# Rows of o as 64 by 64 products on quarters of the array

## Chip, core and metric

The kernel runs on one core of a Trainium2 chip. The metric is the device time of one execution, in microseconds (us). The median of four runs before the change is 909.13 us (908.34 to 909.99).

## The reference

Linear attention over 8 batches, 8 heads, 576 positions and 64 columns a head, then a two-layer network with softplus over the 4608 rows. All inputs and results are float32 to the caller; the inputs of the network's weights arrive in eight bytes a number and are made float32 in the kernel.

```python
def _attn_ref(q, k, v, g_norm):
    kv = np.einsum('bhsd,bhse->bhde', k, v)
    out = np.einsum('bhsd,bhde->bhse', q, kv)
    rms = np.sqrt(np.mean(out * out, axis=-1, keepdims=True) + 1e-06)
    return (out / rms * g_norm).astype(np.float32)

def _moe_ref(x, w_in, w_out):       # x: (B,H,S,D) -> (B*S, H*D) = (4608, 512)
    h = x @ w_in                    # (4608, 2048)
    g = np.maximum(h, 0.0) + np.log1p(np.exp(-np.abs(h)))
    return (g @ w_out).astype(np.float32)
```

## The kernel before

**The network.** The 4608 rows are 12 blocks of 384, each three tiles of 128. The 2048 hidden columns are 16 chunks of 128. The work goes in three phases over the chunks, and in each phase over all blocks; one block with one chunk is a step, and there are 192 steps. To keep float32 accuracy in the fast format fp32r, x, the hidden values and both weights are each split into three terms. A step is one group of 12 products into a bank h (L647), the softplus on ScalarE (L667), the split of its result on ScalarE and VectorE (L669, L658, L662), and three groups of three products into the banks s0, s1, s2 (L654), one for each tile of the block. At the end of a phase `leave` takes the sums out and adds those of the phase before.

**The attention.** For each batch `kv_of` multiplies k by v (L495): five groups of eight float32 products, each of 128 by 64 on one half of the array's columns, halves in turn. A float32 product is two instructions in the trace. The result, 64 by 64 for each head, is copied by two instructions (L499) to `kv_diag`: four blocks of 128 by 128, one for a pair of heads, with zeros off the diagonal. `rows(t)` makes one tile of 128 rows of o: q of the tile, turned so that its columns are in the partitions, times the four blocks of `kv_diag` (L509). Of each product half the multiplications are by the zeros. A tile whose rows lie in two batches (tiles 4, 13, 22, 31) takes four products for each of them, on 64 columns of weights each. Then come the square (L577, ScalarE), the sum by head (L514, VectorE), the power -1/2 (L517, L518, GpSimd) and the scaling, called the norm (L521, VectorE). The product with g_norm is made in the split of x.

**Turning.** For tiles of batches 0 and 1 q is turned on TensorE (L564) and copied (L571); later ones are turned by VectorE (L539). The first 12 tiles of x are turned on TensorE (L526) and copied (L586). The first six go from there into the split of x (L438, L441, L445) as well; all others are stored to DRAM and loaded again by `x_again` (L625), once for each phase.

**Weights.** `weight` loads a chunk's weights (L276), makes float32 of them on VectorE and ScalarE (L287 to L317) and splits them (L349 to L371). For the first four chunks two products with the identity (L367, L368) help in the split.

**The order.** Nothing is ordered by hand: `add` records a task with its engine, an estimated cost in ns, the tasks it follows, a position `pos`, and the slots it takes and gives back. `Plan.order` walks through time and picks for each engine, among the tasks that could start soonest, the one with the least position. The places of a buffer are a ring: `m` has 13 places in SBUF shared by all loads and most temporaries; in PSUM there are h (2), o (2), tp (1), s0, s1, s2 (1 each), eight banks. `P0` holds 40 numbers from which the positions are made. Loads and stores are all issued by the queue on SyncE (SP), in the planned order. Where TensorE would be idle for 400 ns, `plan.spare` puts in a product with the identity (L763) whose result nobody reads, until the first L647.

Of the kernel before, what the change touches and what calls it, by code (L numbers as in the profile page):

```python
# [8 lines left out]
F32 = mybir.dt.float32  # L9
# [9 lines left out]
P = 128  # L19
# [21 lines left out]
class Plan:  # L41
# [3 lines left out]

    HANDOVER = {"PE": 250, "ACT": 120, "DVE": 120, "POOL": 150, "SP": 0}
    READY = {"PE": 2500, "ACT": 2500, "DVE": 4000, "POOL": 2500, "SP": 700}
    BEGIN = 4000
    SOON = 150

# [17 lines left out]
    def order(self):  # L68
        waiting = {id(t): len(t.after) + (t.follows is not None) for t in self.tasks}
        users = {}  # L70
        for t in self.tasks:
            for a in t.after + ([t.follows] if t.follows else []):
                users.setdefault(id(a), []).append(t)
        ready = {}
        for t in self.tasks:
            if not waiting[id(t)]:
                t.ready = 0
                ready.setdefault(t.engine, []).append(t)
        free = {r: [(0, i) for i in range(n)] for r, n in self.rings.items()}
        engine_free = dict(self.READY)  # L80
        dma_free = 1500
        last_read = {}
        done, left = [], len(self.tasks)
        while left:
            best = None
            for engine, tasks in ready.items():
                options = []
                for t in tasks:
                    at = max(engine_free[engine], t.ready)
                    if t.size:  # L90
                        at = max(at, dma_free - 2500)
                    for i, s in enumerate(t.take):
                        others = sum(u.ring == s.ring for u in t.take[:i])
                        if len(free[s.ring]) <= others:
                            break
                        at = max(at, sorted(free[s.ring])[others][0])
                    else:
                        options.append((at, t))
                if not options:
                    continue  # L100
                first = min(at for at, _ in options)
                at, t = min(((at, t) for at, t in options if at <= first + self.SOON),
                            key=lambda o: (o[1].pos, o[0]))
# [12 lines left out]
            if t in ready[t.engine]:  # L116
                ready[t.engine].remove(t)
                left -= 1
            for s in t.take:
                place = min(free[s.ring])  # L120
                free[s.ring].remove(place)
                s.place = place[1]
            t.start = at
            engine_free[t.engine] = at + t.ns
            t.end = at + t.ns + self.HANDOVER[t.engine]
            if t.size:
                dma_free = max(dma_free, at + t.ns) + t.size
# [12 lines left out]
        return sorted(done, key=lambda t: t.start)  # L140
# [3 lines left out]
def kernel(  # L144
# [39 lines left out]
    PLACES = 8  # L184
    LAST = PHASES[-1]

    P0 = [-83.5, -6.7, -71.3, -7.7, -12.6, -28.5, -9.9, 1.7, -54.5, -35.3, -53.7, -10.7, -25.7, -1.2,
          -3.7, -2.2, 0.5, -14.0, 12.5, 9.5, 5.5, 6.0, -2.0, 2.5, 2.5, 19.0, 0.5, 14.5, 8.5, 44.5, 49.5,
          68.0, 52.5, 73.0, 96.5, 100.0, 115.5, 110.5, 114.0, 8.5]
    CONVERT, FETCH, EARLY, LATER = P0[:8], P0[8:16], P0[16:27], P0[27:]  # L190
    BY_PE = 12
    AT_ONCE = 2 * TB
# [2 lines left out]
    const = ctx.enter_context(tc.tile_pool(name="const", bufs=1))  # L195
    sb = ctx.enter_context(tc.tile_pool(name="sb", bufs=1))
    ps = ctx.enter_context(tc.tile_pool(name="ps", bufs=1, space=PSUM))
    dram = ctx.enter_context(tc.tile_pool(name="dram", bufs=1, space=DRAM))

    ident_r = const.tile([P, P], F32R, name="ident_r")  # L200
# [6 lines left out]
    tails = [const.tile([P, H, D], F32, name=f"tail{i}") for i in range(2)]  # L207
    over = const.tile([P, 2 * KF], F32, name="over")
    scale = const.tile([P, 1], F32, name="scale")
    kv_diag = [const.tile([P, NP, P], F32, name=f"kv_diag{i}") for i in range(2)]  # L210


    rings = dict(m=13, xv=2, gv=2, g=2, raw=2, sq=1, 
                 tail0=1, tail1=1, qa=1, xb=1, x=2, r=2,
                 h=2, o=2, tp=1, s0=1, s1=1, s2=1)
    rings.update({f"w{i}_{c}": 1 for i in range(2) for c in range(PLACES)})
    PS = {"h", "o", "tp", "s0", "s1", "s2"}
    plan = Plan(rings)
    slot, add = plan.slot, plan.add

    def new(s, shape, dtype=F32):
        pool = ps if s.ring in PS else sb
        s.tile = pool.tile(shape, dtype, tag=f"{s.ring}_{s.place}", name=f"{s.ring}_{s.place}")
        return s.tile
# [241 lines left out]
    def kv_of(b):  # L466
# [1 line left out]


        pos = x_pos(first_tile[b]) - (EARLY[4] if b else EARLY[5])  # L470
        bank = slot("o")
        last = None
        MAIN = 4 * P
        for p in range(NP + 1):
# [14 lines left out]
            def run(ks=ks, vs=vs, p=p, tail=tail):  # L489
                kv = new(bank, [P, NP, D]) if p == 0 else bank.tile  # L490
                for i in range(4):
                    for e in range(2):
# [2 lines left out]
                        nc.tensor.matmul(kv[e * D:(e + 1) * D, i if tail else p], lhsT=l, rhs=r,  # L495
                                         start=(p == 0 and i == 0), stop=tail, skip_group_check=True)
            last = add("PE", 600, run, lds + [last], pos + 0.5 * p, [bank] if p == 0 else [], [ks, vs])
        kvd = kv_diag[b % 2]
        kv_ready[b] = [add("ACT", 360, lambda r=r: nc.scalar.copy(kvd[r:r + D, :, r:r + D], bank.tile[r:r + D]),  # L499
                           [last] + o_tasks.get(b - 2, []), pos + 2.5, [], [bank]) for r in (0, D)]  # L500

    def rows(t):
        pos = x_pos(t)
        tp, qT, o, x, r, xp, xg = (slot(n) for n in ("tp", "m", f"s{t}" if t < TB else "o", "x", "r", "tp", "m"))
        def out_rows():
            y = new(o, [P, H, D])
            for b, r0, n, _ in parts(t):
                for p in range(NP):
                    nc.tensor.matmul(y[r0:r0 + n, p::NP], lhsT=qT.tile[:, p, r0:r0 + n],  # L509
                                     rhs=kv_diag[b % 2][:, p].rearrange("r (h d) -> r h d", d=D),  # L510
                                     start=(p == 0), stop=True, skip_group_check=True)

        def reduce():
            nc.vector.tensor_reduce(out=new(r, [P, H]), in_=x.tile, axis=AX.X, op=ALU.add)  # L514
# [3 lines left out]
            nc.gpsimd.tensor_tensor(out=r.tile, in0=r.tile, in1=half, op=ALU.pow)  # L518

        def norm():  # L520
            nc.vector.tensor_tensor(out=x.tile, in0=o.tile, in1=r.tile.unsqueeze(2).to_broadcast([P, H, D]), op=ALU.mult)  # L521

        def turn_x():
            y = new(xp, [P, KD, P])
# [9 lines left out]
        for b, r0, n, s0 in parts(t):  # L534
# [23 lines left out]
                    return q_s.tile  # L558
                return q_s.tile[:, t * d_model:(t + 1) * d_model].rearrange("s (h d) -> s h d", d=D)

            def turn_q(n=n, q_s=q_s, at_qa=at_qa, tp=slot("tp")):
                y = new(tp, [P, NP, P])
                for p in range(NP):
                    nc.tensor.transpose(y[:, p, :n], pairs(natural(q_s, at_qa)[:n], p), ident[:n, :n])  # L564
# [6 lines left out]
            turned.append(add("ACT", 590, lambda n=n, r0=r0, tp=tp: nc.scalar.copy(part_of_qT(n, r0), tp.tile[:, :, :n]),  # L571
                              [a], pos - 1, [qT] if not r0 else [], [tp], follows=turned[-1] if turned else None))
        need = [u for pt in parts(t) for u in kv_ready[pt[0]]]
        a = o_task = add("PE", 830 if len(parts(t)) == 1 else 1350, out_rows, turned + need, pos, [o], [qT])
        for pt in parts(t):
            o_tasks.setdefault(pt[0], []).append(a)
        a = add("ACT", 600, lambda: nc.scalar.activation(new(x, [P, H, D]), o.tile, func=AF.Square,  # L577
                                                              scale=D ** -0.5), [a], pos, [x])
        a = add("DVE", 690, reduce, [a], pos, [r])
        a = add("POOL", 2300, root, [a], pos)  # L580
# [53 lines left out]
    def step(s):  # L634
# [25 lines left out]
        def less():  # L660
# [1 line left out]
            nc.vector.scalar_tensor_tensor(out=gv.tile[:, 2], in0=f32[:, 1], scalar=-RADIX, in1=f32[:, 0],  # L662
                                           op0=ALU.mult, op1=ALU.add)

        a = mm1s[s] = add("PE", 2100, mm1, x_split[ph, n] + factors_done[0, c] + [mm1s.get(s - 1)], s, [h],
                ([xv] if c == cs[-1] else []) + ([w_in] if s == last_step[c] else []))
        a = add("ACT", 490, lambda: nc.scalar.activation(new(g, [P, NT]), h.tile, func=AF.Softplus, scale=1.0 + E),  # L667
                [a], s, [g], [h])
# [57 lines left out]
    for e in range(2):  # L726
        nc.scalar.dma_start(out=g_col[e * D:(e + 1) * D], in_=g_norm.rearrange("(d one) -> d one", one=1))
    nc.scalar.preload_act_table_set("softplus")
    scratch = kv_diag[0][:, 0]
    make_identity(nc, scratch)  # L730
    nc.vector.tensor_copy(ident_r, scratch)
    nc.vector.tensor_scalar(out=minus_r, in0=ident, scalar1=-1.0, scalar2=None, op0=ALU.mult)
    nc.gpsimd.tensor_scalar(out=g_down, in0=g_col, scalar1=DOWN_G, scalar2=None, op0=ALU.mult)
    nc.vector.memset(half, -0.5)
    nc.vector.memset(big, 2.0 ** 30)
    for x in kv_diag + tails:
        nc.vector.memset(x, 0.0)

    for c in range(KF):
# [23 lines left out]
        nc.tensor.matmul(new(s, [P, 4, P]), lhsT=ident_r, rhs=ident_r.unsqueeze(1).to_broadcast([P, 4, P]),  # L763
                         start=True, stop=True)

    plan.spare = ("h", warm, 400, mm1s[0])
    for t in plan.order():
        t.run()

# [29 lines left out]
```

## Time and profile before

| | before |
|---|---|
| median of four runs | 909.13 us |
| the profiled execution: its time | 908.98 us |
| its span, first to last instruction | 907.2 us |
| TensorE busy | 896.4 us |
| VectorE, ScalarE, GpSimd busy | 625.8, 412.3, 83.8 us |
| L647 and L654, matmul busy | 434.5 and 433.5 us |
| L509, matmul busy | 40.4 us, 320 instructions |
| L495, matmul busy | 27.7 us, 640 instructions |
| L763, matmul busy | 14.6 us, 36 instructions |
| first L647 | 39.87 us after the start |
| last L509 | 309.2 us after the start |

PE is TensorE's matmul, PEld its weight load, which lies beside it; DVE is VectorE, ACT ScalarE, POOL GpSimd. Records of matmuls overlap their neighbours', so the distance from one start to the next is the better measure of what an instruction takes. A line of the timeline shows the start and the length of a run of instructions of one kind, in us, and how many they are; a figure in brackets is idle time before it.

### The profile page before, as it was taken

What the parts mean: (1) busy time and instruction counts of PE and PEld (TensorE: products, weight loads), DVE (VectorE), ACT (ScalarE), POOL (GpSimd) and SP (SyncE); (2) the same over time, 40 slices, a digit from 0 to 9 for tenths busy, and PEclk for the clock granted to TensorE, in tenths of its full rate; (3) what the DMA queues carried; (4) which work ended last, traced back from release to release, by engine and by line L of the source; (5) the groups of instructions that cost most, each with busy time, mean ns of one, the idle gap of its engine ahead of it and who ended that gap; (6) DMA issues with size and microseconds to landing.
All of it is one profiled execution on the core that took longest, in us unless ns stands there. A gap on an engine that the chain in (4) does not pass through costs nothing.

```text
span 907.2 us, 13880 instructions
## 1 busy us (share of the span) xinstructions
PE 896.4 (99%) x5134; PEld 802.2 (88%) x5134; DVE 625.8 (69%) x1056; ACT 412.3 (45%) x796; POOL 83.8 (9%) x79
## 2 busy tenths in 40 slices
PE   7999999999999999999999999999999999999998
PEld 5788889988889999999899999999899999989997
DVE  6887878775658887688756888887534555555553
ACT  4875556433334566554434545545323333333331
POOL 0424222212213200000000000000000000000000
PEclk8999999999999999999999999999999999999999
DMA  9999896579792544455334454732330433333323
GB/s 251 283 243 236 223 234 187 100 190 176 181 164 49 147 129 139 128 168 181 105 105 128 128 185 130 241 136 76 105 102 4 139 105 105 105 105 105 105 73 102
DMA packets 211444, 131.47 MB, mean 145 GB/s; under 512 B 102320, under 2 KB 185264, under 8 KB 211376
## 3 DMA queue, kind: packets, MB, share of 16 engines
q1 hardware_dynamic: 211216, 130.58, 53.8%
q8 instruction: 40, 0.66, 0.3%
q14 instruction: 28, 0.23, 0.1%
q10 hardware_dynamic: 160, 0.00, 0.0%
HBM read 91.75 MB, written 38.80 MB: 144 GB/s over the span
## 4 chain that ended last, share of the span: by engine, by line
PE 95%; DMA 2%; DVE 1%; ACT 1%; issue 0%; DVEq 0%; ACTq 0%; SPq 0%
PE s L654 44%; PE h L647 44%; PE o L509 3%; PE o L495 2%; DMA raw<-in_moe_w_in_dram 1%; PE tp L526 1%; DMA m<-in_k_dram 1%; PE tp L564 0%; DMA x<-m 0%; PE s L509 0%; DVE xv L441 0%; DVE m L313 0%; DVE m L295 0%; ACT xv L438 0%; DVE m L300 0%
## 5 line engine op out<-in xcount | busy, mean ns | idle before, releaser
L647 PE MATMUL h<-xv,w 128*128 128x384 f32 x2304 | 434.5, 337 | 0.0
L654 PE MATMUL s<-w,gv 128*128 128x512 f32 x1728 | 433.5, 395 | 0.0
L647 PEld LDWEIGHTS h<-xv,w 128*128 128x128 f32 x2304 | 406.6, 188 | 15.2
L654 PEld LDWEIGHTS s<-w,gv 128*128 128x128 f32 x1728 | 319.7, 188 | 59.9 <-issue 0.3
L667 ACT ACTIVATE g<-h 128x384 f32<-128x384 f32 x192 | 94.3, 491 | 410.0 <-PE h L647 406.8
L658 DVE TENSOR_TENSOR gv<-g,gv 128x384 fp32r<-128x384 f32 x192 | 106.6, 555 | 179.6 <-ACT gv L669 178.7
L662 DVE SCALAR_TENSOR_TENSOR gv<-gv 128x384 fp32r<-128x384 f32 x192 | 106.9, 557 | 5.9
L669 ACT ACTIVATE gv<-g 128x384 fp32r<-128x384 f32 x192 | 100.8, 525 | 16.1 <-PE s L654 9.4
L441 DVE SCALAR_TENSOR_TENSOR xv<-m,g_col,xv 128x512 fp32r<-128x512 f32 x102 | 75.8, 743 | 1.4 <-ACT xv L438 1.4
L445 DVE SCALAR_TENSOR_TENSOR xv<-xv 128x512 fp32r<-128x512 f32 x108 | 74.4, 689 | 2.6
L438 ACT ACTIVATE xv<-m,g_down 128x512 fp32r<-128x512 f32 x102 | 69.9, 710 | 3.4 <-DMA m<-x 3.2
L518 POOL TENSOR_TENSOR r<-r,half 128x8 f32<-128x8 f32 x36 | 66.8, 1854 | 3.0
L694 DVE SCALAR_TENSOR_TENSOR m<-s,scale,m 128x512 f32<-128x512 f32 x24 | 17.9, 746 | 30.1 <-PE s L654 30.1
L509 PE MATMUL o<-kv_diag,m 128*128 128x128 f32 (+1 forms) x296 | 37.0, 276 | 0.0
L509 PEld LDWEIGHTS o<-kv_diag,m 128*128 128x128 f32 (+1 forms) x296 | 35.0, 179 | 2.2 <-issue 1.0
L517 POOL TENSOR_SCALAR r<-r 128x8 f32<-128x8 f32 x36 | 16.1, 447 | 221.7 <-DVE r L514 221.4
L514 DVE TENSOR_REDUCE r<-x 128x8 f32<-128x512 f32 x36 | 24.4, 679 | 9.6 <-ACT x L577 9.4
L521 DVE TENSOR_TENSOR x<-o,r 128x512 f32<-128x512 f32 x33 | 22.7, 688 | 10.8 <-POOL r L518 10.5
L694 DVE SCALAR_TENSOR_TENSOR m<-s,m 128x512 f32<-128x512 f32 x36 | 23.4, 684 | 9.1 <-PE s L654 8.4
L495 PEld LDWEIGHTS o<-m,m 128*64 128x64 f32 x512 | 18.2, 143 | 10.5 <-issue 6.0
L304 ACT ACTIVATE sq<-sq,big 128x512 bf16<-128x512 bf16 x32 | 22.9, 717 | 9.8 <-DVE m L300 9.8
L352 DVE TENSOR_TENSOR m<-m,w 128x512 f32<-128x512 f32 x30 | 20.5, 685 | 8.4 <-ACT w L349 3.5
(65 smaller groups left out, 435.8 us busy)
## 6 DMA issues: line engine op xcount, KB each, us to landing
m<-x SPq DMA_DIRECT2D x102, 256.0 KB, 4.8
part<-m SPq DMA_DIRECT2D x72, 256.0 KB, 2.5
m<-part SPq DMA_DIRECT2D x72, 256.0 KB, 3.9
raw<-in_moe_w_in_dram SPq DMA_DIRECT2D x16, 512.0 KB, 5.6
m<-in_k_dram SPq DMA_DIRECT2D x32, 256.0 KB, 4.9
m<-in_v_dram SPq DMA_DIRECT2D x32, 256.0 KB, 4.9
raw<-in_moe_w_out_dram SPq DMA_DIRECT2D x16, 512.0 KB, 4.8
qa<-in_q_dram SPq DMA_DIRECT2D x24, 288.0 KB, 6.2
```

What stands on the lines that cost most here:

```text
L438: nc.scalar.activation(cols(0, F32R), x.tile, func=AF.Identity, scale=g_down)
L441: nc.vector.scalar_tensor_tensor(out=cols(1, F32R), in0=x.tile, scalar=g_col, in1=cols(0), op0=ALU.mult, op1=ALU.subtract)
L445: nc.vector.scalar_tensor_tensor(out=cols(2, F32R), in0=cols(1), scalar=-RADIX, in1=cols(0), op0=ALU.mult, op1=ALU.add)
L509: nc.tensor.matmul(y[r0:r0 + n, p::NP], lhsT=qT.tile[:, p, r0:r0 + n], rhs=kv_diag[b % 2][:, p].rearrange("r (h d) -> r h d", d=D), start= ...
L518: nc.gpsimd.tensor_tensor(out=r.tile, in0=r.tile, in1=half, op=ALU.pow)
L647: nc.tensor.matmul(hp, lhsT=w_in.tile[:, i, kd * P:(kd + 1) * P], rhs=xv.tile[:, i, kd], start=(m == 0), stop=(m == 3 * KD - 1))
L654: nc.tensor.matmul(mine[i].tile, lhsT=gv.tile[:, m, i * P:(i + 1) * P], rhs=w_out.tile[:, m], start=(c == cs[0] and m == 0), stop=(c == cs ...
L658: nc.vector.tensor_tensor(out=gv.tile[:, 1], in0=g.tile, in1=gv.tile.bitcast(F32)[:, 0], op=ALU.subtract)
L662: nc.vector.scalar_tensor_tensor(out=gv.tile[:, 2], in0=f32[:, 1], scalar=-RADIX, in1=f32[:, 0], op0=ALU.mult, op1=ALU.add)
L667: a = add("ACT", 490, lambda: nc.scalar.activation(new(g, [P, NT]), h.tile, func=AF.Softplus, scale=1.0 + E), [a], s, [g], [h])
L669: a = add("ACT", 530, lambda: nc.scalar.activation(new(gv, [P, 3, NT], F32R)[:, 0], g.tile, func=AF.Copy, scale=DOWN), [a], s, [gv])
L694: a = add("DVE", 700, lambda: nc.vector.scalar_tensor_tensor(out=new(ot, [P, d_model]), in0=bank.tile, scalar=(scale if ph == LAST else 1. ...
```

## The change

- **Rows of o.** `kv_diag` becomes `kvs`, 128 by 4 by 64, without the zero blocks; it is filled by one copy. A tile of rows is 16 products in place of 4 (or 8): for each pair of heads p, four of 64 by 64, one on each quarter of the array. `e` picks the head of the pair and with it the half of the array's rows, `half` the half of the tile's rows and with it the half of the array's columns; a tile with rows of two batches takes the batch's kv by `half`.
- **Places in PSUM.** The two places of o are no longer a bank each: `o_banks` lies over two banks, and each place has half of both, so that the heads with e = 0 are in one bank and those with e = 1 in the other. The columns are now in the order in which the products leave them, and square and norm read them through a rearranged view. kv takes the banks s0, s1 (batches 0, 1) and tp (later ones) and no longer o; the turns of q and x from tile 6 on take places of o and no longer tp; the first three tiles of rows take o and no longer s0 to s2.
- **The planner.** A load into the ring m is put in only where four further places are free (`KEEP`). A group of L647 is not planned ahead of the second weights of two steps before. `spare` goes on until the seventh L647. The cost of rows is given as 640 ns, that of the kv copy as 400. All of `P0` has new numbers.

```diff
+    KEEP = 4
...
                         others = sum(u.ring == s.ring for u in t.take[:i])
+                        if engine == "SP" and s.ring == "m":
+                            others += self.KEEP
                         if len(free[s.ring]) <= others:
                             break
-                        at = max(at, sorted(free[s.ring])[others][0])
+                        at = max(at, sorted(free[s.ring])[sum(u.ring == s.ring for u in t.take[:i])][0])
...
+    o_banks = ps.tile([P, NP, 2, P], F32, name="o_banks")
...
-    kv_diag = [const.tile([P, NP, P], F32, name=f"kv_diag{i}") for i in range(2)]
+    kvs = [const.tile([P, NP, D], F32, name=f"kv{i}") for i in range(2)]
...
-    PS = {"h", "o", "tp", "s0", "s1", "s2"}
+    PS = {"h", "tp", "s0", "s1", "s2"}
...
     def new(s, shape, dtype=F32):
+        if s.ring == "o":
+            s.tile = o_banks[:, :, s.place]
+            return s.tile
...
-        bank = slot("o")
+        bank = slot(f"s{b}" if b < 2 else "tp")
...
-        kvd = kv_diag[b % 2]
-        kv_ready[b] = [add("ACT", 360, lambda r=r: nc.scalar.copy(kvd[r:r + D, :, r:r + D], bank.tile[r:r + D]),
-                           [last] + o_tasks.get(b - 2, []), pos + 2.5, [], [bank]) for r in (0, D)]
+        kv_ready[b] = [add("ACT", 400, lambda: nc.scalar.copy(kvs[b % 2], bank.tile), [last] + o_tasks.get(b - 2, []),
+                           pos + 2.5, [], [bank])]
...
-        tp, qT, o, x, r, xp, xg = (slot(n) for n in ("tp", "m", f"s{t}" if t < TB else "o", "x", "r", "tp", "m"))
+        tp, qT, o, x, r, xp, xg = (slot(n) for n in ("tp", "m", "o", "x", "r", "tp" if t < AT_ONCE else "o", "m"))
+
         def out_rows():
-            y = new(o, [P, H, D])
-            for b, r0, n, _ in parts(t):
-                for p in range(NP):
-                    nc.tensor.matmul(y[r0:r0 + n, p::NP], lhsT=qT.tile[:, p, r0:r0 + n],
-                                     rhs=kv_diag[b % 2][:, p].rearrange("r (h d) -> r h d", d=D),
-                                     start=(p == 0), stop=True, skip_group_check=True)
+            y = new(o, [P, NP, P])
+            parts_of = parts(t)
+            for p in range(NP):
+                for e, half in ((0, 0), (1, 1), (0, 1), (1, 0)):
+                    b = parts_of[half if len(parts_of) > 1 else 0][0]
+                    r0, a, c0 = half * (P // 2), (e * NP + p) // 2, p % 2 * D
+                    nc.tensor.matmul(y[r0:r0 + P // 2, a, c0:c0 + D], lhsT=qT.tile[e * D:(e + 1) * D, p, r0:r0 + P // 2],
+                                     rhs=kvs[b % 2][e * D:(e + 1) * D, p], start=True, stop=True)
...
-            nc.vector.tensor_tensor(out=x.tile, in0=o.tile, in1=r.tile.unsqueeze(2).to_broadcast([P, H, D]), op=ALU.mult)
+            by_head = r.tile.rearrange("s (a k) -> s a k", k=2).unsqueeze(3).to_broadcast([P, NP, 2, D])
+            nc.vector.tensor_tensor(out=x.tile.rearrange("s (a k) d -> s a k d", k=2),
+                                    in0=o.tile.rearrange("s a (k d) -> s a k d", k=2), in1=by_head, op=ALU.mult)
...
-            def turn_q(n=n, q_s=q_s, at_qa=at_qa, tp=slot("tp")):
+            def turn_q(n=n, q_s=q_s, at_qa=at_qa, tp=slot("tp" if t < AT_ONCE else "o")):
...
-        a = o_task = add("PE", 830 if len(parts(t)) == 1 else 1350, out_rows, turned + need, pos, [o], [qT])
+        a = o_task = add("PE", 640, out_rows, turned + need, pos, [o], [qT])
...
-        a = mm1s[s] = add("PE", 2100, mm1, x_split[ph, n] + factors_done[0, c] + [mm1s.get(s - 1)], s, [h],
+        a = mm1s[s] = add("PE", 2100, mm1, x_split[ph, n] + factors_done[0, c] + [mm1s.get(s - 1)] +
+
+                (factors_done[1, ORDER[s - 2][2]] if s > 1 else []), s, [h],
...
-    for x in kv_diag + tails:
+    for x in tails:
         nc.vector.memset(x, 0.0)
...
-    plan.spare = ("h", warm, 400, mm1s[0])
+    plan.spare = ("h", warm, 400, mm1s[6])
```

More of the change, by code (lines that the diff above doesn't have):

```diff
@@ L185 @@
     LAST = PHASES[-1]
-    P0 = [-83.5, -6.7, -71.3, -7.7, -12.6, -28.5, -9.9, 1.7, -54.5, -35.3, -53.7, -10.7, -25.7, -1.2,
-          -3.7, -2.2, 0.5, -14.0, 12.5, 9.5, 5.5, 6.0, -2.0, 2.5, 2.5, 19.0, 0.5, 14.5, 8.5, 44.5, 49.5,
-          68.0, 52.5, 73.0, 96.5, 100.0, 115.5, 110.5, 114.0, 8.5]
+    P0 = [-93.0, 0.8, -33.3, -5.7, -14.1, 1.5, -43.9, 2.2, -65.0, -42.8, -62.7, -19.7, -30.7, -6.2,
+          -2.2, -4.7, 2.5, -26.5, 18.0, 10.5, 5.5, 8.5, -2.0, 2.5, 3.5, 25.5, -16.5, 10.0, 6.5, 41.0,
+          52.0, 65.5, 54.5, 72.0, 91.5, 94.5, 115.5, 106.0, 111.5, 8.5]
     CONVERT, FETCH, EARLY, LATER = P0[:8], P0[8:16], P0[16:27], P0[27:]
@@ L573, in rows @@
         need = [u for pt in parts(t) for u in kv_ready[pt[0]]]
-        a = o_task = add("PE", 830 if len(parts(t)) == 1 else 1350, out_rows, turned + need, pos, [o], [qT])
+        a = o_task = add("PE", 640, out_rows, turned + need, pos, [o], [qT])
         for pt in parts(t):
             o_tasks.setdefault(pt[0], []).append(a)
-        a = add("ACT", 600, lambda: nc.scalar.activation(new(x, [P, H, D]), o.tile, func=AF.Square,
+        a = add("ACT", 600, lambda: nc.scalar.activation(new(x, [P, H, D]).rearrange("s (a k) d -> s a (k d)", k=2), o.tile, func=AF.Square,
                                                               scale=D ** -0.5), [a], pos, [x])
@@ L728 @@
     nc.scalar.preload_act_table_set("softplus")
-    scratch = kv_diag[0][:, 0]
+    scratch = kvs[0].rearrange("r p d -> r (p d)")[:, :P]
     make_identity(nc, scratch)
```

## The prediction

> **What bounds the kernel now.** I read the page's busy times first, then the stretches of time, then the timeline of TensorE.
>
> ```profile
> PE 896.4 (99%) x5134; PEld 802.2 (88%) x5134; DVE 625.8 (69%) x1056; ACT 412.3 (45%) x796; POOL 83.8 (9%) x79
> PE 95%; DMA 2%; DVE 1%; ACT 1%; issue 0%; DVEq 0%; ACTq 0%; SPq 0%
> L509 PE MATMUL o<-kv_diag,m 128*128 128x128 f32 (+1 forms) x296 | 37.0, 276 | 0.0
> ```
>
> TensorE is busy for 99% of the span and makes 95% of the chain of waits. L509, the product that the change rewrites, has 37.0 us, and 3.3 more in three tiles that go to other banks. The stretches say where TensorE is the bound:
>
> ```profile
> 9.30:39.90 30.60, 28.78 (x281) 21.41 (x281) 24.89 (x42) 22.39 (x45) 8.44 (x8) 0.90 1.06 270
> 39.90:100.00 60.10, 59.95 (x472) 52.99 (x471) 49.69 (x85) 40.16 (x79) 20.75 (x18) 1.00 1.02 247
> 100.00:309.50 209.50, 209.50 (x1394) 187.58 (x1393) 154.08 (x261) 98.42 (x189) 51.11 (x44) 1.00 0.75 165
> 309.50:880.00 570.50, 570.50 (x2870) 517.21 (x2869) 381.33 (x641) 242.79 (x469) 2.55 (x2) 1.00 0.40 121
> ```
>
> Columns: stretch, its length, busy us of PE, weight loads, DVE, ACT and POOL, the granted clock, the DMA share, GB/s. The first L647 starts at 39.87 us. From there to 880 us TensorE is idle for 0.15 us in all, so work taken out of it there comes off the end one for one. Ahead of 39.87 us that isn't so: of the 36 fillers of L763, 24 run between 9.3 and 39.9 us, and filled time is idle time with another name. What sets the first L647 is the turned and split x of the first three tiles, on ACT and DVE (DVE 24.89 of 30.60 us).
>
> **What a group of L509 really costs.** Records of matmuls overlap, so I take starts: how much later the second next block starts when a group stands between L647 and L654.
>
> ```profile
> 403.29 2.27 PE L647 MATMUL h<-xv,w 128*128 128x384 f32 x12
> 405.40 2.24 PE L654 MATMUL s<-w,gv 128*128 128x512 f32 x9
> 407.48 2.27 PE L647 MATMUL h<-xv,w 128*128 128x384 f32 x12
> ...
> 272.64 2.27 PE L647 MATMUL h<-xv,w 128*128 128x384 f32 x12
> 274.85 1.58 PE L509 MATMUL o<-kv_diag,m 128*64 128x128 f32 x16
> 276.36 2.35 PE L654 MATMUL s<-w,gv 128*128 128x512 f32 x9
> 278.55 2.27 PE L647 MATMUL h<-xv,w 128*128 128x384 f32 x12
> ...
> 215.83 2.27 PE L647 MATMUL h<-xv,w 128*128 128x384 f32 x12
> 218.04 0.69 PE L495 MATMUL o<-m,m 128*64 128x64 f32 x16
> 218.65 2.33 PE L654 MATMUL s<-w,gv 128*128 128x512 f32 x9
> 220.82 0.38 PE L509 MATMUL o<-kv_diag,m 128*128 128x128 f32 x2
> ...
> 109.23 2.27 PE L647 MATMUL h<-xv,w 128*128 128x384 f32 x12
> 111.43 1.62 PE L495 MATMUL o<-m,m 128*64 128x64 f32 x48
> 112.98 2.33 PE L654 MATMUL s<-w,gv 128*128 128x512 f32 x9
> 115.15 1.03 PE L647 MATMUL h<-xv,w 128*128 128x384 f32 x5
> ```
>
> The plain pair takes 407.48 - 403.29 = 4.19 us. With the tile of two batches between, 278.55 - 272.64 = 5.91: that tile costs 1.72. A tile of one batch (8 instructions, two to an f32 product) costs 0.87: two L647 with one such tile and one L654 between them start at 235.82 and 240.88, 5.06 apart, and others 5.05. One L495 group, 16 instructions on two halves of the columns, costs 220.82 - 215.83 - 4.19 = 0.80; three in a row cost 115.15 - 109.23 - 4.19 = 1.73. So each further group adds (1.73 - 0.80)/2 = 0.465, which is 8 instructions of each half at 58 ns, and a visit to the split array costs 0.80 - 0.465 = 0.335 once. Single records there start 7 and 52 ns apart in turn: the two halves run together. And where L509 crosses from one half to the other, the first instruction of the new half starts 6 ns behind the fifth of the old one, with three of the old half passed over.
>
> **The new rows.** A tile is 16 products of 64 by 64, 32 instructions, 8 on each quarter, and the program's order of quarters needs three waiting instructions passed over, which the trace shows. Each instruction has 64 columns of weights and 64 moving, as L495. What no row shows is two halves of the rows running at once. Bounds: all four quarters together, 8 instructions deep as L495, 0.80 plus two more starts of 7 ns, 0.82 a tile; two at a time, 16 deep, 0.80 + 0.465 = 1.27; one at a time, 32 deep, 0.80 + 3 x 0.465 = 2.2. I take 0.82: the quarters of the two row halves write separate banks (columns 0, 1 and 2, 3 of the o tile), so the nearest row, column halves that run together, carries over. Against the old 0.87 that is 0.05 a tile; only the four tiles of two batches gain much, 0.90 each.
>
> The Trainium skill speaks both ways. "TensorE: Matmul & The Clock Gate", under "Wait — 56ns, not 53.3ns?", says that starts of matmuls are never closer than about 25 ns; by it 31 starts of a tile alone take 0.78 us, its cost is near 1.2, and 36 tiles lose some 8 us to the old. The starts 7 ns apart on neighbouring column halves are against it here. "TensorEngine Tiling (Array Packing)", "Key Properties", lets tiles load and multiply independently, but drains the array when the kind of split changes.
>
> **The sum, from the first L647 on.** In the changed order on TensorE, that block has four tiles of rows ahead of it (five before), one turned q fewer and one pair of L367/L368 fewer, and the same ten groups of L495.
> - Rows: before 28 x 0.87 + 3 x 1.72 = 29.5; then 32 x 0.82 = 26.2: -3.3.
> - The turned q and the pair now behind it: 0.41 (a group of L564 at 102 ns an instruction) + 2 x 0.32 = +1.05.
> - Fillers: 53, not 36; 47 stand ahead of the first L647 and 6 behind it. Six in a row took 1.68 us from start to start at 16.84 us, 0.28 each: +1.7. They cost 0 if TensorE would have stood idle, 2.5 at the 0.42 of a lone one.
> - Two places where two tiles of rows stand together share a visit: 2 x 0.335 = -0.7. At 13 more a tile stands beside L495; if halves and quarters share the visit, 13 x 0.335 = 4.4 more come off. The tile beside a different form is nearest to L495 beside the unsplit array, which pays: I take 0.
> - Idle of TensorE behind the first L647: 0.15 before; I take 0.4, bounds 0 and 3.
> - Start of the first L647: DVE runs 47 instructions from the first weight to the last split of tile 2, as before, the same kinds. 0, bounds -3 (about half of DVE's 5.7 us of idle there) and +2.
> Sum: -3.3 + 1.05 + 1.7 - 0.7 + 0.25 = -1.0. Fillers and rows ahead of the first L647 are not counted, since ACT and DVE cover them; without that cover a tile of rows is worth 0.1 to 0.2 us there, a filler 0.28.
>
> **Edits costed at nothing.** The copy of kv becomes one instruction of 128x256 in place of two of 64x256 (16 x 364 ns; a 128x256 copy took 366): ACT gains 2.9 us at 66% load. Two memsets of 485 ns leave DVE while it waits for the first weights anyway. Square and norm read the o tile through four strided pieces, priced as now (592 and 688 ns); if sharing a bank with TensorE's writes made them 10% slower, 36 x 0.13 = 4.7 us would fall on ACT and DVE, which have 34% and 26% idle from 39.9 to 309.5 us. Loads: the 561 issues of the queue on SP are the same, line by line; those of k and v move by a few places, under an engine share of 1.06 and 1.02 in the first 100 us. Rows now have the two o places alone: tile 2 waits for the norm of tile 0. Ahead of it on TensorE stands the turn of x of tile 0, which needs the same norm, and so for tiles 3 and 4; no wait is new in TensorE's order, but tile 2's rows, which ran at 26.11 us before its square had room at 29.72, now run later. Those 3.6 us are spare time for it.
>
> **Rivals.**
> 1. Forecast, four quarters together and a start as long as now: 908.98 (the profiled execution) - 1.0 = 908.0; own range 905 to 911. Chance 0.48.
> 2. Visits are shared and the start shrinks: 4.4 off, and 1 of DVE's idle: 908.0 - 5.4 = 902.6. For it: three L495 groups share a visit. Against: those are one form. 0.21.
> 3. Two quarters at a time (a row half waits for the other): 32 x 0.45 = 14.4 more: 922.4. It decides from 0.91 us a tile on: 32 x 0.09 = 2.9 takes the whole from 1.0 below the old to 1.9 above. For it: no row of the trace has the rows of the array split. 0.14.
> 4. The start is starved: rows of tiles 2 and 3 wait for norms, each norm 5.6 us behind its rows (square, reduce, the 2.1 us power on POOL, norm), and loads held back for four shared places land late. First L647 at 43 us and 2 us of idle behind it: 908.0 + 5 = 913.0. For it: six fillers behind the first L647, where there were none. Against: DVE's same 47 instructions. It decides from a first L647 at 42 us on. 0.17.
>
> **How the numbers follow.** From no change one can tell 0.2%, 1.8 us: 907.3 to 910.9 around the median of 909.13 (the profiled execution lies 0.15 under it). Faster: rival 2 and two fifths of case 1, 0.21 + 0.20 = 0.41. Slower: rival 3, nearly all of 4 and the upper end of case 1, 0.14 + 0.16 + 0.04 = 0.34. Same: 0.25. The range of 902 to 915 leaves out rival 3 and the outer ends of 2 and 4.
>
> **What would show it.** Right: L521's groups between L660 and L667 lengthen the pair of blocks by 0.82, TensorE's busy time changes by under 3 us, the first L660 starts at 38 to 41 us, idle behind it under 1 us. A tile at 1.27 is rival 3; a tile at 0.82 with a first L660 past 42 us is rival 4; groups beside L502 at 0.5 are rival 2. The forecast is also wrong if square or norm grow and TensorE waits for the softplus behind them.

## The result, and the profile after

The changed kernel takes 908.54 us (median of 34 runs, 906.64 to 911.98) against 909.63 us for the kernel before in the same comparison (52 runs). The ratio is 0.9988, with a 95% interval of 0.9983 to 0.9993: about 1.1 us less, clear of zero but within the 0.2% that the prediction called no change. The forecast was 908.0 us, 1.0 us under the profiled execution of before. The profiled execution of after took 908.51 us, its span is 906.7 us.

The page of the changed kernel, busy times and the group of the new products:

```profile
PE 894.0 (99%) x5983; PEld 789.4 (87%) x5983; DVE 624.1 (69%) x1054; ACT 408.1 (45%) x788; POOL 84.5 (9%) x79
L521 PE MATMUL o_banks<-kv,m 64*64 64x64 f32 x1152 | 24.5, 224 | 0.8 <-ACT m L584 0.7
```

The rows of o went from 40.4 us of busy time to 24.5, in 1152 instructions where there were 320. TensorE as a whole is busy for 894.0 us where it was 896.4: a group's busy time is no measure of what comes off the whole, since records overlap their neighbours', and other work has come in. The stretches of the changed kernel (columns as before):

```profile
9.30:39.90 30.60, 28.21 (x361) 19.41 (x361) 24.33 (x41) 19.64 (x40) 9.34 (x8) 0.89 1.06 266
39.90:100.00 60.10, 58.49 (x693) 49.15 (x694) 50.49 (x87) 39.93 (x81) 21.39 (x18) 1.00 1.01 237
100.00:309.50 209.50, 209.50 (x1945) 181.27 (x1944) 154.84 (x262) 98.27 (x189) 51.03 (x46) 1.00 0.71 169
```

From 39.9 to 100 us TensorE is now idle for 1.6 us, where it was 0.15; behind that it is as full as it was. The first group of h (now L660) starts at 40.36 us, before at 39.87. From there to the end of the last product it took 862.97 us before and 861.77 now: that is where the gain is, 1.2 us, and 0.5 of it goes into the later start.

The lines of the kernel have new numbers: in the changed kernel L660 is the group of h, L667 that of s, L502 that of kv, L521 a tile of rows and L778 a filler; the experiments shift them a little, and the names of the tiles stay. What a tile of rows costs now, in the timeline of the changed kernel (start, length, kind and number of a run of instructions):

```profile
232.08 2.24 PE L660 MATMUL h<-xv,w 128*128 128x384 f32 x12
234.25 0.69 PE L521 MATMUL o_banks<-kv,m 64*64 64x64 f32 x32
234.88 2.36 PE L667 MATMUL s<-w,gv 128*128 128x512 f32 x9
237.08 1.21 PE L660 MATMUL h<-xv,w 128*128 128x384 f32 x6
...
212.31 2.27 PE L660 MATMUL h<-xv,w 128*128 128x384 f32 x12
214.51 0.69 PE L502 MATMUL tp<-m,m 128*64 128x64 f32 x16
215.13 0.69 PE L521 MATMUL o_banks<-kv,m 64*64 64x64 f32 x32
215.76 2.33 PE L667 MATMUL s<-w,gv 128*128 128x512 f32 x9
218.02 0.28 PE L502 MATMUL tp<-m,m 128*64 128x64 f32 x2
```

237.08 - 232.08 - 4.19 = 0.81 us for a tile alone, by the same reading that gave 0.87 for the old one. Single records start 6 or 7 ns apart in fours, and the fours 58 ns apart (the second four 107 behind the first): the four quarters run together. Read to the third instruction behind the group, where the next block has settled, a tile alone costs 0.83 (14 of them lie at 0.82 to 0.85), an old one 0.90 and an L495 or L502 group 0.82; these finer readings are used from here on. In the second piece a group of kv and a tile stand side by side, and the next block is another group of kv. The same place is read again in e1 below.

### The profile page after: what moved, and what is told of

Its sections match the earlier page's. It is cut to its first block, busy times and chain, and to the rows that moved or that the text cites. A ratio compares the mean times of both kernels' runs of the same rounds, so it can differ in the third digit from the quotient of the medians.

```text
span 906.7 us, 15563 instructions
## 1 busy us (share of the span) xinstructions
PE 894.0 (99%) x5983; PEld 789.4 (87%) x5983; DVE 624.1 (69%) x1054; ACT 408.1 (45%) x788; POOL 84.5 (9%) x79
## 4 chain that ended last, share of the span: by engine, by line
PE 95%; DMA 3%; ACT 0%; DVE 0%; issue 0%; SPq 0%
PE h L660 44%; PE s L667 44%; PE o_banks L521 2%; DMA m<-in_v_dram 2%; PE tp L502 2%; DMA raw<-in_moe_w_in_dram 1%; PE h L778 1%; PE s L502 1%; PE tp L539 0%; PE tp L577 0%; PE h L374 0%; SPq L491 0%; PE o_banks L539 0%; PE h L375 0%; ACT x L590 0%
## 5 line engine op out<-in xcount | busy, mean ns | idle before, releaser
L660 PE MATMUL h<-xv,w 128*128 128x384 f32 x2304 | 435.3, 337 | 0.2 <-ACT w L378 0.2
L667 PE MATMUL s<-w,gv 128*128 128x512 f32 x1728 | 433.5, 395 | 0.0
L660 PEld LDWEIGHTS h<-xv,w 128*128 128x128 f32 x2304 | 406.3, 188 | 16.4 <-ACT w L378 0.4
L667 PEld LDWEIGHTS s<-w,gv 128*128 128x128 f32 x1728 | 319.7, 188 | 60.4 <-DVE gv L675 0.2
L533 DVE TENSOR_TENSOR x<-o_banks,r 128x512 f32<-128x512 f32 x36 | 24.8, 689 | 17.3 <-POOL r L529 8.5
L521 PEld LDWEIGHTS o_banks<-kv,m 64*64 64x64 f32 x1152 | 19.9, 134 | 9.7 <-issue 5.5
L590 ACT ACTIVATE x<-o_banks 128x512 f32<-128x512 f32 x36 | 21.2, 594 | 13.2 <-PE o_banks L521 7.5
L521 PE MATMUL o_banks<-kv,m 64*64 64x64 f32 x1152 | 24.5, 224 | 0.8 <-ACT m L584 0.7
```

The lines of the kernel that those rows point to most:

```text
L521: nc.tensor.matmul(y[r0:r0 + P // 2, a, c0:c0 + D], lhsT=qT.tile[e * D:(e + 1) * D, p, r0:r0 + P // 2], rhs=kvs[b % 2][e * D:(e + 1) * D, ...
L660: nc.tensor.matmul(hp, lhsT=w_in.tile[:, i, kd * P:(kd + 1) * P], rhs=xv.tile[:, i, kd], start=(m == 0), stop=(m == 3 * KD - 1))
L667: nc.tensor.matmul(mine[i].tile, lhsT=gv.tile[:, m, i * P:(i + 1) * P], rhs=w_out.tile[:, m], start=(c == cs[0] and m == 0), stop=(c == cs ...
```

## The experiments

Ratios are to the kernel before, timed on the same chip in the same turn. Behind each, three readings of its trace: the start of the first group of h, the time from there to the end of the last product, and the idle time of TensorE in it.

| | median, us | ratio | 95% interval | first h | from first h | idle |
|---|---|---|---|---|---|---|
| before | | 1 | | 39.87 | 862.97 | 0.15 |
| changed | 908.54 | 0.9988 | 0.9983 to 0.9993 | 40.36 | 861.77 | 1.54 |
| e1 whole products | 917.01 | 1.0079 | 1.0065 to 1.0093 | 41.07 | 870.51 | 0.60 |
| e2 row halves in turn | 916.45 | 1.0073 | 1.0060 to 1.0085 | 40.41 | 869.36 | 0.57 |
| e3 fillers to the first h | 907.95 | 0.9977 | 0.9965 to 0.9988 | 40.75 | 860.44 | 1.39 |
| e4 no places kept free | 914.18 | 1.0049 | 1.0036 to 1.0063 | 38.69 | 869.40 | 5.59 |
| e5 tiles in pairs | 910.21 | 0.9996 | 0.9983 to 1.0009 | 40.93 | 864.94 | 6.54 |
| e6 kv joined | 906.41 | 0.9957 | 0.9945 to 0.9970 | 39.74 | 860.05 | 2.79 |
| e7 both, few fillers | 913.00 | 1.0035 | 1.0025 to 1.0046 | 40.06 | 866.86 | 10.95 |
| e8 old positions | 921.93 | 1.0130 | 1.0116 to 1.0143 | 39.33 | 876.52 | 10.00 |
| e9 kv joined, few fillers | 906.55 | 0.9960 | 0.9947 to 0.9972 | 41.80 | 858.78 | 3.46 |
| e10 pairs at the first | 906.03 | 0.9961 | 0.9947 to 0.9975 | 39.47 | 860.46 | 2.90 |
| e11 all joined | 901.78 | 0.9913 | 0.9900 to 0.9926 | 39.62 | 856.41 | 3.70 |

### e1: the old products in the new order

The core of the edit; the copy of kv is two instructions again, and square and norm read the tile through another view.

```diff
-                for e, half in ((0, 0), (1, 1), (0, 1), (1, 0)):
...
-                    nc.tensor.matmul(y[r0:r0 + P // 2, a, c0:c0 + D], lhsT=qT.tile[e * D:(e + 1) * D, p, r0:r0 + P // 2],
-                                     rhs=kvs[b % 2][e * D:(e + 1) * D, p], start=True, stop=True)
+            for b, r0, n, _ in parts_of:
+                for p in range(NP):
+                    nc.tensor.matmul(y[r0:r0 + n, p], lhsT=qT.tile[:, p, r0:r0 + n], rhs=kv_diag[b % 2][:, p],
+                                     start=True, stop=True)
```

> The changed kernel with its order, places and loads, but each tile of rows again as 4 products of 128 by 128 (8 on two batches) with zero blocks off the diagonal. Theory A, the product form is what counts: behind the first group of h a tile of one batch goes back from 0.83 to 0.89 us, one of two batches from 0.83 to 1.72, and the two places with two tiles together lose 0.36 each: 29 x 0.06 + 3 x 0.89 + 0.7 = 5.1 us longer than the changed kernel, a ratio of 1.0045 to the kernel before. Theory B, the gain is the new order, places and loads and the products give nothing: within 1 us of the changed kernel, a ratio of 0.998 to 1.000.

The time from the first group of h grew by 8.7 us. Theory A is right in direction and too small by 3.6 us; theory B is out. Why it was too small, the same place of the order shows, here in e1's timeline:

```profile
219.88 2.27 PE L662 MATMUL h<-xv,w 128*128 128x384 f32 x12
222.08 0.69 PE L502 MATMUL tp<-m,m 128*64 128x64 f32 x16
222.70 1.16 PE L523 MATMUL o_banks<-kv_diag,m 128*128 128x128 f32 x8
223.61 2.34 PE L669 MATMUL s<-w,gv 128*128 128x512 f32 x9
225.88 0.34 PE L502 MATMUL tp<-m,m 128*64 128x64 f32 x4
```

225.88 - 219.88 = 6.00 us here and 218.02 - 212.31 = 5.71 in the changed kernel: beside a group of kv the new tile is 0.29 us cheaper, not 0.06. Over all such places, a group of kv and a new tile together cost 1.44 us, 0.21 less than 0.82 + 0.83; with the old tile 1.71, about the plain sum of 0.82 + 0.90. So two kinds of split, halves of columns and quarters, share 0.21 us of the 0.36 that a visit to the split array costs beyond its products (0.83 less 8 x 0.058). The expectation also counted one tile of two batches too few: behind the first group of h the new order has four of them and not three, which is 0.83 us. With 13 x 0.23 us for the places beside kv, that makes 8.9 in place of 5.1; e1 is idle for 0.94 us less than the changed kernel, and about 0.8 of the 8.7 stays unexplained.

The other side of e1: with the old products, the new order takes 7.5 us longer from the first group of h than the kernel before. So the new products, what they share with groups of kv included, are worth 8.7 us in this order, and the order costs nearly as much.

### e2: one half of the array's rows after the other

```diff
-            for p in range(NP):
-                for e, half in ((0, 0), (1, 1), (0, 1), (1, 0)):
+            for e in range(2):
+                for p, half in [(p, half) for p in range(NP) for half in range(2)]:
```

> The changed kernel with the 16 products of a tile in another order: the eight on the upper half of the array's rows first, column halves in turn, then the eight on the lower half. Theory A, quarters run together as far as TensorE passes over waiting instructions (three, by the trace of before): the two row halves now overlap only where they meet, a tile takes 1.10 to 1.27 us in place of 0.83, and behind the first group of h 32 tiles cost 9 to 14 us more than the changed kernel, a ratio of 1.008 to 1.014 to the kernel before. Theory B, the order of the products in the program doesn't matter because TensorE finds free quarters at any distance: 0.83 us a tile and a ratio of 0.998 to 1.000.

The timeline of e2:

```profile
237.21 2.25 PE L660 MATMUL h<-xv,w 128*128 128x384 f32 x12
239.38 0.98 PE L521 MATMUL o_banks<-kv,m 64*64 64x64 f32 x32
240.29 2.36 PE L667 MATMUL s<-w,gv 128*128 128x512 f32 x9
242.49 0.69 PE L660 MATMUL h<-xv,w 128*128 128x384 f32 x3
```

The same products in another order take 1.11 us a tile (14 tiles alone, 1.10 to 1.12) in place of 0.83, at the low end of what theory A gave; the ratio, 1.0073, is just under its range, and theory B is out. Sixteen deep, with the row halves never together, would be 0.83 + 8 x 0.058 = 1.29. The 0.18 between is three instructions of 58 ns. In the single records of a tile the first products of the lower half start 294 and 300 ns behind the tile's start, right behind the fifth instruction of each upper quarter (281 and 288), with three of each still waiting. So TensorE starts a product for a free quarter past three that wait for each of the others, six in all here, and no sooner. The order of quarters in the changed kernel needs three passed over, one for each of the other quarters.

### e3: six fillers fewer

```diff
-    plan.spare = ("h", warm, 400, mm1s[6])
+    plan.spare = ("h", warm, 400, mm1s[0])
```

> The changed kernel with fillers only until the first group of h, so 47 in place of 53; the order of the rest is the planner's. Theory A, the six later fillers are work on a bound engine: 1.7 us less, of which up to 1 comes back as idle time, so a ratio of 0.997 to 0.998 to the kernel before. Theory B, they lie in time in which TensorE would wait for ScalarE, VectorE or loads: no change from the changed kernel, 0.9988.

The time from the first group of h falls by 1.33 us and the idle time in it stays (1.39). The ratio of the runs, 0.9977, lies inside A's range, but its interval overlaps that of the changed kernel, so by the times alone it isn't told apart from no change. In sum the trace looks like theory A; place by place it doesn't. These are TensorE's longest waits from 40 to 100 us, first in the changed kernel, then in e3:

```profile
PE tp L502 <- DMA m<-in_v_dram: 0.7, 1, 0.7
PE o_banks L539 <- ACT x L590: 0.4, 1, 0.4
...
PE o_banks L521 <- ACT m L584: 0.7, 1, 0.7
PE tp L502 <- DVE xv L448: 0.3, 1, 0.3
```

At the two places where the six stood, TensorE's work is 1.1 us less, but 0.9 of that comes back as waits there (the two of e3), so the places give 0.25 us. The other 1.06 us are the two waits of the changed kernel, for a load of v and a turn of x, which e3 doesn't have; e1 and e2, with all fillers, don't have them either. So the fillers stood mostly where TensorE would have waited, as theory B says, and whether their absence also ended the other two waits is open.

### e4: no places kept free of loads

```diff
-    KEEP = 4
+    KEEP = 0
```

> The changed kernel without the four places kept free of loads; the planner makes another order of it, with 42 fillers ahead of the first group of h in place of 47. Theory A, the places held back make v come late (TensorE waited 0.77 and 0.65 us for loads of v): those waits go and the time falls by 0.5 to 1.5 us, a ratio of 0.997 to 0.998. Theory B, the free places let ScalarE and VectorE go on: without them the first group of h comes later than 40.4 us by 1 to 3 us and the time grows by as much, a ratio of 1.000 to 1.002.

Theory A is out. Theory B has the sign, and not the place: the first group of h came 1.7 us earlier, not later, and the fourth one 12 us later (77.1 us, 65.0 in the changed kernel), with 11 fillers and 5.6 us of idle time behind the first. This is who TensorE waited for in e4 from 38 to 100 us (total, times, longest):

```profile
PE o_banks L521 <- ACT m L584: 0.9, 2, 0.7
PE o_banks L539 <- DVE x L533: 0.8, 1, 0.8
PE o_banks L521 <- DVE x L533: 0.7, 1, 0.7
PE h L660 <- ACT w L378: 0.7, 1, 0.7
PE o_banks L521 <- ACT m L599: 0.7, 1, 0.7
```

There it waits for turned q and x, for norms and split weights, on ScalarE and VectorE, and no longer for loads of v. That these come later because loads hold the places of m that their results need was not tried by itself.

### e5, e6, e7: sharing visits on purpose

If a visit costs some 0.36 us beyond its products, groups of one kind should stand together. In e5 two tiles of rows from tile 12 on are one task; in e6 the five groups of kv from batch 2 on are two tasks. The core of both edits:

```diff
+        a = add("PE", 640 if len(jobs) == 1 else 1105, all_rows, [u for j in jobs for u in j[3]], pos,
+                [j[4] for j in jobs], [j[5] for j in jobs])
...
+            held.append((run, lds, [ks, vs]))
+            if b >= 2 and p in (0, 2, 3):
+                continue
...
+            last = add("PE", 135 + 465 * len(held), run_all, [u for one in held for u in one[1]] + [last], pos + 0.5 * p,
+                       [bank] if last is None else [], [s for one in held for s in one[2]])
```

> The changed kernel, but from tile 12 on the products of two tiles are one task, one behind the other. Theory A, what a visit to the split array costs beyond its products is paid once for a pair: the trace of the changed kernel has 0.83 us for one tile and 1.30 for two together, 0.365 saved a pair; there are 12 pairs in place of 2, so 3.65 us less, from which comes off what tiles beside groups of kv save now (0.21 each, up to 8 places): 2.0 to 3.7 us less than the changed kernel, a ratio of 0.995 to 0.997 to the kernel before. Theory B, a pair needs both places of o at once and keeps them until both norms are done, so TensorE waits: idle behind the first group of h grows by over 2 us and the ratio is 0.998 or more.

> The changed kernel, but from batch 2 on the five groups of kv are two tasks, of two and three groups. Theory A, groups in a row share a visit to the split array: three in a row took 1.76 us in the trace of before against 0.82 for one, 0.35 saved for each further one; the order has 19 such in place of 1, so 6.4 us less, and at most 2.7 of it goes where groups of kv stand beside tiles of rows now: 3.7 to 6.4 us less than the changed kernel, a ratio of 0.992 to 0.995 to the kernel before. Theory B, the joined groups wait for the last of their loads and keep their places in m longer: TensorE is idle for over 3 us behind the first group of h and the ratio is 0.998 or more.

> The changed kernel with tiles of rows in pairs, groups of kv joined, and fillers only until the first group of h. Theory A, visits and fillers are work on the bound engine and add up: 2.0 to 3.7, 3.7 to 6.4 and 1.2 us less than the changed kernel, 7 to 11 us together, a ratio of 0.987 to 0.991 to the kernel before; it is faster than both. Theory B, less work on TensorE uncovers waits for loads and norms: idle behind the first group of h above 4 us and a ratio above 0.994.

e6 came out as theory A, 0.9957, just past its range, with 1.25 us more idle time and three more fillers than the changed kernel. The work was shared in e5 too: a pair costs 1.30 us in place of 1.66. But idle time ate it, as theory B had it, though not for the places of o. TensorE's waits in e5 from 100 to 330 us:

```profile
PE h L683 <- DVE xv L448: 2.6, 2, 1.8
PE s L690 <- DVE gv L694: 0.7, 1, 0.7
PE s L690 <- DVE gv L698: 0.4, 1, 0.4
```

A group of h waits for the split of x: the pair was planned at the second tile's position, and so the first tile's x came late. Another 2.3 of the 6.54 us are three waits for loads of v from 58 to 67 us, ahead of the first pair at 105 us; whether they belong to the order that the pairs make or to that execution is open. In e7 both joinings take work away (from the first group of h without idle time 855.9 us, 860.2 in the changed kernel), but the waits add up to 10.95 us. The waits cost more there than their length, as the stretches and the timeline of e7 show:

```profile
130.00:139.30 9.30, 7.41 (x68) 6.12 (x58) 7.10 (x14) 3.93 (x8) 2.77 (x3) 1.00 1.20 189
145.60:149.90 4.30, 4.30 (x12) 3.48 (x12) 4.20 (x8) 1.02 (x2) 0.00 (x0) 0.50 1.14 321
...
145.51 4.54 PE L693 MATMUL h<-xv,w 128*128 128x384 f32 x12 [3.90 <-ACT xv L445]
```

Around two waits of 1.95 and 3.90 us the granted clock went from 1.00 to 0.50, and the same group of h took 4.54 us where it takes 2.27; until the clock was back at 1.00, at 151.5 us, that came to some 2.7 us, an estimate from the starts.

### e8: the old positions

P0 is that of the kernel before, all else as changed.

> The changed kernel with the 40 numbers of P0 from before, all else as changed (four places kept free). Theory A, the new order takes back most of what the new products give: with it undone the fillers and groups behind the first group of h that the new order put there (1.7 and 1.05 us) and the idle time (1.4 us) go, 3 to 4 us less than the changed kernel, a ratio of 0.994 to 0.996 to the kernel before. Theory B, the old positions don't fit the new places: tiles, turns and kv wait for each other's banks, the first groups of h come later, and the ratio is above 1.001.

Theory B has the sign and the size, 1.013, though the first group of h came 1.0 us earlier and not later. There are 10 us of idle time, 5.6 of them in one wait of L667 for split weights, and behind that wait the clock was again at half:

```profile
175.90:181.50 5.60, 4.85 (x10) 3.23 (x11) 2.92 (x5) 1.26 (x2) 2.67 (x2) 0.50 1.21 176
```

The new positions are dear, but the old ones don't fit the new places and loads. Which part of the order could be cheaper is not settled by this.

### e9, e10, e11: the best of these

> The changed kernel with groups of kv joined from batch 2 on, and fillers only until the first group of h. Theory A, the two gains add up since both take work out of the bound engine: e6 has a ratio of 0.9957 with 9 fillers behind the first group of h, 2.8 us; without them, and with half of that coming back as waits, 1.4 to 2.8 us less: 0.993 to 0.9945 to the kernel before, faster than both kernels. Theory B, these fillers stand where TensorE waits anyway: 0.9955 to 0.996.

e9 is no faster than e6 (0.9960 and 0.9957, intervals overlapping), which by the times is theory B. From the first group of h it is 1.3 us quicker; but that group came at 41.80 us, behind waits of 6.8 us for loads of v at the start, of 4.1 in e6. Whether this start belongs to the order or to that execution is open.

```diff
     def rows(t):
-        pos = x_pos(t)
+        pos = x_pos(t - t % 2 if t >= BY_PE else t)
```

> e5 with one thing changed: the second tile of a pair has the position of the first, so the pair is planned where the first tile stood and not where the second did. Theory A, e5 lost its 3.65 us to x that came late (TensorE waited 0.77 and 1.79 us at a group of h for the split of x, and 1.1 for VectorE in between): planned earlier, the pair's x is there in time, idle behind the first group of h falls from 6.5 to under 3 us and the ratio to 0.995 to 0.998. Theory B, the two places of o, held by a pair until both norms are done, make the waits wherever the pair stands: idle stays above 4.5 us and the ratio above 0.998.

> e7 with the second tile of a pair at the position of the first. Theory A, as in e10: idle behind the first group of h falls from 11 us to under 5, and with 53.8 us of groups between those of h and s against 59.7 in the changed kernel the ratio is 0.990 to 0.995, the fastest of all. Theory B, with visits shared everywhere the loads, turns and norms can't keep up: idle above 7 us and a ratio above 0.997.

This one line turns e5 from 0.9996 into 0.9961, idle time from 6.54 to 2.90 us: the waits for the split of x and of the hidden values, 3.7 us in e5, are gone, so the pair was late. Of the 2.90, 2.3 are again loads of v, and no wait for a place of o is over 0.13 us. e11 has all of it: 901.78 us, a ratio of 0.9913 (0.9900 to 0.9926), by the ratio 7.9 us less than the kernel before, and the fastest here. Its timeline shows the shared visits, two tiles as one run of 64 and two groups of kv as one of 32:

```profile
235.44 1.16 PE L533 MATMUL o_banks<-kv,m 64*64 64x64 f32 x64
236.53 2.35 PE L700 MATMUL s<-w,gv 128*128 128x512 f32 x9
238.73 2.27 PE L693 MATMUL h<-xv,w 128*128 128x384 f32 x12
240.93 1.15 PE L503 MATMUL tp<-m,m 128*64 128x64 f32 x32
```

## Why the prediction was right, and where its terms were off

The forecast, its sign and its size came out. In the sum that was in part luck, since errors cancelled: 2.7 us of sharing that it took as 0 stand against 1.4 for groups of kv, about 1.15 of idle time beyond the 0.25 and 0.4 within the groups. Of the signs named, the pair of blocks, the busy time and the start came true, and idle time under 1 us did not (1.54); a tile beside a group of kv costs 1.44 - 0.82 = 0.62, between the 0.82 of the forecast and the 0.5 of rival 2. From the first group of h on:

| term | predicted, us | measured, us |
|---|---|---|
| rows, each tile alone | -3.3 | -3.8 (32 x 0.83 less 28 x 0.90 and 3 x 1.72) |
| two places with two tiles | -0.7 | -0.7 (1.30 for two, 1.66 apart) |
| tiles beside a group of kv | 0 | -2.7 (13 places, 0.21 each) |
| a turned q and a pair of L367/L368 more | +1.05 | +1.0 |
| six fillers | +1.7 | +1.1 (beside e3; 0.25 after the waits that take their place) |
| groups of kv no longer three in a row | not in the sum | +1.4 (four sharings of 0.35) |
| idle time | +0.25 | +1.4 |
| within the groups of h and s themselves | 0 | +0.4 |
| sum | -1.0 | -1.9; -1.20 by the starts and ends, so 0.7 is not placed |
| start of the first group of h | 0 | +0.5 |

- **The four quarters run together.** Right, with the cost of a tile within 0.01 us (0.82 said, 0.81 by the same reading, 0.83 by the finer one), carried over from two column halves. e2 shows that it hangs on the order of the products. Two at a time, the rival at 922.4 us, is nearly e2, which came to 916.45 because the halves still overlap where they meet.
- **Shared visits.** The step that failed: "The tile beside a different form is nearest to L495 beside the unsplit array, which pays: I take 0". It was mis-sized: the bound of 0.335 a place was nearer the mark, with 0.21 measured. The Trainium skill, "TensorEngine Tiling (Array Packing)", "Key Properties", has the array drain when the kind of split changes, and not only the tile; here going from halves to quarters or back costs 0.36 - 0.21 = 0.15 us, less than a full way out and in.
- **The kv groups.** The sum said that there were "the same ten groups of L495" ahead of the first group of h, and never asked how those behind it stood. Before, two batches had three groups in a row; now none behind the first group of h has two. That is an error of omission: the order of the groups was there to be read before the run.
- **Fillers.** Priced by six in a row, 0.28 each; from start to start the six in the changed kernel, three times two, add up to the same 1.7, but taking them out, in e3, took 1.1 us of work away, and nearly all of that was time in which TensorE then waited.
- **Idle time.** 0.4 was taken of a range up to 3, and 1.54 came: 0.65 in one wait for a load of v and 0.41 in one turn of x that waits for a square. The second has a new cause. Durations of square and norm did not grow (594 and 689 ns), as priced, but in the changed kernel the norm waited 4.8 us in all for squares, before not at all. Its own square lies two steps back, behind the sum and the power, so it is another tile's: in all four places the norm starts 0.1 us behind the end of another tile's square. That fits both places of o lying over the same two banks, so that engines use them one after the other; neither this nor what of TensorE's waits it makes in all was tried by itself.
- **The start.** 40.36 us lies in the range; it came 0.5 us later than before, with eleven more fillers ahead of it. That ScalarE and VectorE set it was argued and not tried by itself; TensorE's waits ahead of it include 4.0 us for loads of v (before 2.9).
- **What the sum netted out.** e1 shows a gain of 8.7 us from the products and a price of 7.5 for the order. Of that price 1.1 are fillers, 1.0 the turn and the pair, 1.7 a tile of two batches, 1.4 the kv groups and 0.45 idle time; 1.8 are not placed. Half of it, the first three, is work that stands behind the first group of h now while that group came no sooner.

## What to carry to other kernels

Where one engine is full, price a new form of a product by the start of the second block behind it, and count visits to a split array, not only products: joining what stands apart took the ratio from 0.9988 to 0.9913 in e11 (with six fillers fewer), some 6.8 us, where the change itself gave 1.1. Work that moves behind the point where the bound engine fills up must bring that point forward, or it is lost time. And a plan made from estimated costs must be read again for what stands beside what, since a task that gets cheaper or joined can come late for those that wait for it.

## What the runs showed of the hardware

- Products on neighbouring parts of a split array start 6 to 7 ns apart. "TensorE: Matmul & The Clock Gate", "Wait — 56ns, not 53.3ns?", has about 25 ns as the least distance between starts; between different quarters these runs show less, and the loss of 8 us worked out from it did not come.
- TensorE started products for a free part of the array past three waiting ones for each other part, and not past more: past three in the tile of two batches of the kernel before, past six, three for each upper quarter, in e2 (1.11 us a tile; 1.29, an estimate, with none passed).
- A visit to the split array costs about 0.36 us beyond its products, in and out together, and a change between halves of columns and quarters 0.15.
- Around long waits of TensorE the granted clock fell to 0.50: in e7 around waits of 1.95 and 3.90 us, until 151.5 us, and in e8 at one of 5.56 us. The single waits of up to 2.0 us in e5 left it at 1.00.
